# A gated attention and token mixer on one core: heads once a batch in 64x64 tiles, the last row group from transposed blocks, casting loads, and another end

## The chip, the core and the metric

The kernel runs on one core of a Trainium2 chip. TensorE (PE) multiplies matrices into PSUM; PEld is its loading of weights. VectorE (DVE), ScalarE (ACT) and GpSimd (POOL) work on elements, and SyncE (SP) issues most DMAs. The metric is the time of one execution on the device in microseconds, the median of several runs.

## The reference

Two stages for 8 batches of S = 3200 rows with D = 256; z has 64 columns and d_hyper is 64:

```python
scores = (1/S) * z @ z.T                    # per batch, 3200 x 3200, symmetric
x = u * (np.maximum(scores, 0.0) ** 2 @ v)  # 3200 x 256
wq, wk = x @ w_q, x @ w_k                   # 3200 x 64 each
W_tok = (1/8) * wq @ wk.T                   # 3200 x 3200
mixed = W_tok @ x
out = np.maximum(mixed, 0.0) @ w_out        # 3200 x 256
```

The second stage has no nonlinearity between `wq`, `wk` and `x`, so `mixed` is computed as `wq @ (wk.T @ x)`. The 64x256 matrix `wk.T @ x` of a batch is called its heads.

## The kernel before

**Tiling.** A batch has 25 row tiles of 128 rows, in seven row groups: six of four tiles (512 rows, groups 0 to 5) and a last one of a single tile (group 6, `LASTG`). The attention block of row group gi against row tile ti is computed transposed: `scores` multiplies z by z (64 rows of contraction, so two blocks run on the two row halves of TensorE at once) into the PSUM tile `sc`; `first_stage` takes the positive part into `g` on DVE or ACT; `second_stage` squares it into the fp16 tile `at` on POOL or ACT. Eleven `at` tiles go round. `second_product` multiplies `at` by `v` and adds up in `acc` (two banks), and `gate` multiplies by `u` into `x_sb`.

**Symmetric blocks.** The scores are symmetric, so some blocks are not computed but turned: `is_turned(gi, gj)` names pairs of groups of which the block of gi is transposed by a DMA on SP's queue (`second_stage`, the tile `tt`) and used for gj. Before, these are the next two groups, and group 4 for group 0; the last group has none and computes all its 25 blocks, four of 128x128 to a PSUM bank.

**Steps.** A main loop runs in steps (`k`). A step makes the scores of up to three pairs of blocks, runs the element stages of the pairs of the step before, and adds 4 to 25 row tiles into `acc`. Into this stream other work is woven: a call for keys (`keys_and_heads`), a mix (`mix`, TensorE tile `mx`), or an output projection (`project`, tile `fo`). The order is written by the program: `key_due`, `mix_due` and `shares` decide what goes into which step, and `at_phase` holds the loads that are due at a step. Most matmuls are cut into two of 64 rows of contraction, one for each row half (lane), in two passes so that each lane uses one PSUM bank at a time (`first_pass`, `second_pass`). Where there are no new scores left, near the end, matmuls are whole.

**Second stage.** `turn_x` transposes `x` by DMA. `keys_and_heads` makes queries and keys of a group (512 columns into one bank), `turn_keys` transposes the keys by DMA into `kx`, whose other 64 columns are zero. In a later key call `heads` multiplies the keys of a group that is done by its x, in the other bank, and `heads_out` adds the part to `ha` on DVE. After the last group of a batch the heads are copied to both halves (`spread_heads`), and six mixes and the projections of the batch are put into the steps of the next batches. The last group's mix and projection ride in key calls (`side_mix`, `side_proj`).

**Loads.** `load_piece` loads a piece of `v` or `z` in fp32 on SP's queue into `piece` and, some steps later, POOL and ACT in turn cast it to fp16 (`asides`). Only the first batch's `v` is loaded by casting DMAs of POOL's queue. `u` is loaded and the output stored on SP's queue.

**End.** The order after the last step is a list of words (`ENDING`). The last two groups' heads don't wait for turned keys: the Gram product of x (`last_gram`, tile `xtx`) is copied to fp32 and multiplied by w_k (`last_heads`).

Of the kernel before, what the change touches and what calls it, by code (L numbers as in the profile page):

```python
# [16 lines left out]
def kernel(  # L17
# [24 lines left out]
    LAG = 2  # L42
    FAR = 2
# [30 lines left out]
    def acc_tile(half, name, dtype=FP32):  # L74
# [9 lines left out]
        f00s H G g0A g1D f01 L F004AS f10s f11 F104AS h f20a q0s m01 m00 r00A F202DS r01D f21  # L84
        m10 q1a r10A m11 p00s F222DS p01 P002DS r11A p10a p11 P102DS P122DS P022AS m20 r20A
        p20s p21 m21 P204DS r21A p30s p31 P304DS s0a p40s p41 P422DS P402AS p60s P601AS p50a
        p51 P502AA P522DS
# [52 lines left out]
    def load_piece(k, b, src, dst, n0, nn, later):  # L140
        d = src.shape[2]
        piece = pst.tile([P, nn, d], FP32, tag="piece", name="piece")
        nc.sync.dma_start(out=piece[:], in_=rows(src, b)[:, n0 : n0 + nn, :])

        def cast():
            copy = nc.gpsimd.tensor_copy if now[0] % 2 == 0 else nc.scalar.copy
            copy(out=dst()[:, n0 : n0 + nn, :], in_=piece[:])

        due(k + later, lambda: asides.append(cast))
# [6 lines left out]
    def load_z(k, b, n0, nn):  # L156
        load_piece(k, b, z, lambda: zr, n0, nn, 4)

# [39 lines left out]
    wk2 = consts.tile([P, ND, 2, dh], FP32, tag="wk2", name="wk2")  # L198
    wo = consts.tile([P, ND, D], FP16, tag="wo", name="wo")
    zeros = consts.tile([P, P], FP16, tag="zeros", name="zeros")  # L200
    kxs = [pk.tile([P, 4, 2, dh], FP16, tag=f"kx{i}", name=f"kx{i}") for i in range(4)]
# [31 lines left out]
    def is_turned(gi, gj):  # L233
        return gi < gj < LASTG and (gj <= gi + FAR or (gi, gj) == (0, 4))

# [10 lines left out]
    for b in range(B):  # L246
        for gi in range(NG):
            near = [t for t in range(NT) if is_turned(gi, group_of(t))]
# [55 lines left out]
    def second_stage(p0, g, on_act):  # L304
# [15 lines left out]
        for b, gi, gj, n0, nn, c0, c1 in blocks:  # L320
            if (b, gi, gj) not in turned:
                bufs = {1: 3, 2: 4, 4: 1}[gj - gi]
                turned[b, gi, gj] = ptt.tile(
                    [P, 4, 4, P], FP16, tag=f"tt{gj - gi}", name=f"tt{gj - gi}", bufs=bufs
                )
# [140 lines left out]
    def gate(b, gi):  # L466
# [14 lines left out]
        else:  # L481
            if nn > 2:
# [3 lines left out]
            if nn > 2:  # L486
                nc.gpsimd.tensor_mul(out=x[:, n : 2 * n], in0=upper[:], in1=ug[:, n : 2 * n])  # L487
        to_turn.append((b, gi))
# [13 lines left out]
    def projections(b, gi, w, out, start=True):  # L502

        gw = widths[gi]
        return [
            Item(
                out=out,
                lhsT=lambda r, ac=ac: w[r, ac, :, :].rearrange("p t h -> p (t h)"),
                rhs=lambda r, ac=ac: xTs[b, gi][r, 0 : gw // P, ac, :],
# [3 lines left out]
            for ac in range(ND)  # L513
        ]

    def projections_out(b, gi, out):
# [5 lines left out]
        nc.scalar.copy(out=qks[b, gi][:, 0:gw], in_=out)  # L522
# [14 lines left out]
    def heads(b, gis, ps, stop=True):  # L537

        parts = [(gi, n) for gi in gis for n in range(widths[gi] // P)]
        return [  # L540
            Item(
                out=ps[:, 1, 0:D],
                lhsT=lambda r, gi=gi, n=n: ks[b, gi][r, n, :, :].rearrange("p a h -> p (a h)"),
                rhs=lambda r, gi=gi, n=n: xs[b, gi][r, n, :],
                start=((gi, n) == parts[0]),
                stop=(stop and (gi, n) == parts[-1]),
            )
            for gi, n in parts
        ]

    def heads_out(b, gis, ps):
        if gis[0] == 0:
            hacc[b] = psml.tile([P, D], FP32, tag="ha", name="ha")
            nc.vector.tensor_copy(out=hacc[b][0:dh, :], in_=ps[0:dh, 1, 0:D])
        elif gis[-1] < LASTG:
            nc.vector.tensor_add(
                out=hacc[b][0:dh, :], in0=hacc[b][0:dh, :], in1=ps[0:dh, 1, 0:D]
            )
        else:
            heads_done(b, ps[:, 1, 0:D], spread=False)  # L560
            to_spread.append(b)

    def spread_heads(b):
        nc.scalar.copy(out=hss[b][dh:P, :], in_=hss[b][0:dh, :])
        nc.scalar.copy(out=hz[b % 2][dh:P, :], in_=hss[b][0:dh, :])

    def heads_done(b, part, spread=True):
        hss[b] = psml.tile([P, D], FP16, tag="hs", name="hs")
        nc.vector.tensor_add(out=hss[b][0:dh, :], in0=hacc.pop(b)[0:dh, :], in1=part[0:dh, :])
        if spread:  # L570
            nc.vector.tensor_copy(out=hss[b][dh:P, :], in_=hss[b][0:dh, :])

# [370 lines left out]
    while groups:  # L943
# [34 lines left out]
        if mixing:  # L978
            mix_out(*mixing)
# [281 lines left out]
```

## Time and profile before

| | us |
|---|---|
| median of 3 runs | 780.81 |
| lowest and highest | 778.7, 783.08 |
| profiled execution, from first to last instruction | 776.9 |
| mean granted TensorE clock in it | 0.998 |

For the profiled execution the page gives the span; its own time, with what lies around the span, isn't listed apart from the runs, which are 1.8 to 6.2 us above that span.

How to read the lines of a profile: `L347 PE MATMUL acc<-v_sb,at 64*128 64x256 f16 x7334 | 472.5, 269 | 1.9 <-...` is a group of instructions: line of the kernel, engine, operation, output and inputs by the program's names, the weights' and the moving operand's form, the count; then busy microseconds and the mean nanoseconds of one; then the idle time of the engine just before them and what ended it. Matmuls are pipelined, so the length of one is longer than the distance to the next. A line of a timeline is start, length, and the instructions merged in it. `PEclk` is the granted share of the TensorE clock. The share of DMA is packet time over that of 16 engines and can go over 1. Line numbers are those of the kernel whose profile it is.

### The profile page before, as it was taken

The numbers are of one execution on the slowest core, as the hardware profiler recorded it, in microseconds if no ns is written. First come the engines' busy times: TensorE is split into PE (matmuls) and PEld (weight loads), VectorE is DVE, ScalarE is ACT, GpSimd is POOL, SyncE is SP. The second block draws the span as 40 slices with busy tenths as digits, with TensorE's granted clock in tenths as the row PEclk, the third lists the DMA queues.
The fourth block names the chain that finished last, engine by engine and source line by source line (L and its number), as shares of the span: only waits on it lengthen the run. The fifth ranks groups of instructions, "written<-read, shape, count | busy, mean of one in ns | idle before, by whom it ended". The sixth has DMA issues, their size and how long they took to land.

```text
span 776.9 us, 28324 instructions
## 1 busy us (share of the span) xinstructions
PE 765.0 (98%) x12542; PEld 629.3 (81%) x12542; DVE 474.0 (61%) x459; ACT 558.4 (72%) x657; POOL 554.1 (71%) x361
## 2 busy tenths in 40 slices
PE   9999999999999999999999999999999999999996
PEld 6777877888788988888888887888888888988884
DVE  7654676546765577555766457655585646665444
ACT  8666787777778787685867667758687878685465
POOL 7897797768766678766879668886777546875450
PEclk9999999999999999999999999999999999999999
DMA  8899799987999679994999949999489995987726
GB/s 186 176 202 227 141 212 173 191 181 125 213 220 216 133 188 204 234 229 134 189 224 231 220 131 203 226 202 242 115 210 187 217 236 112 206 190 160 161 65 259
DMA packets 276554, 147.03 MB, mean 189 GB/s; under 512 B 252112, under 2 KB 255696, under 8 KB 276432
## 3 DMA queue, kind: packets, MB, share of 16 engines
q1 hardware_dynamic: 275712, 143.33, 87.8%
q0 software_dynamic: 576, 1.64, 1.1%
q8 instruction: 98, 1.61, 0.9%
q14 instruction: 24, 0.20, 0.1%
q10 hardware_dynamic: 144, 0.26, 0.1%
HBM read 59.38 MB, written 26.21 MB: 110 GB/s over the span
## 4 chain that ended last, share of the span: by engine, by line
PE 92%; DVE 2%; ACT 2%; POOL 1%; DMA 1%; issue 1%; ACTq 0%; DVEq 0%; POOLq 0%
PE acc L347 67%; PE sc L285 12%; PE qk L347 6%; PE fo L347 5%; PE mx L600 1%; POOL at L310 1%; DMA tt<-at 1%; DVE g L299 1%; DVE x_sb L485 1%; ACT at L308 1%; DVE fo L1219 0%; ACT g L297 0%; DMA z<-in_z_dram 0%; ACT gt L484 0%; DVE zT L136 0%
## 5 line engine op out<-in xcount | busy, mean ns | idle before, releaser
L299 DVE TENSOR_SCALAR g<-sc 128x1024 f32<-128x1024 f32 x337 | 410.1, 1223 | 242.1 <-PE sc L285 220.8
L310 POOL TENSOR_TENSOR at<-g 128x1024 f16<-128x1024 f32 x238 | 448.1, 1893 | 122.2 <-DVE g L299 93.6
L347 PE MATMUL acc<-v_sb,at 64*128 64x256 f16 (+1 forms) x7387 | 479.5, 269 | 2.0 <-DVE x_sb L485 0.7
L347 PEld LDWEIGHTS <-at 64*128 64x128 f16 (+1 forms) x7387 | 370.2, 94 | 84.3 <-PE acc L347 24.5
L308 ACT ACTIVATE at<-g 128x1024 f16<-128x1024 f32 x230 | 239.3, 1055 | 27.2 <-DVE g L299 16.0
L347 PE MATMUL acc<-v_sb,tt 64*128 64x256 f16 (+1 forms) x2540 | 179.2, 269 | 0.0
L285 PE MATMUL sc<-zT 64*128 64x512 f16 (+1 forms) x1104 | 170.3, 345 | 0.9 <-DVE g L299 0.5
L297 ACT ACTIVATE g<-sc 128x1024 f32<-128x1024 f32 x131 | 134.1, 1023 | 41.6 <-PE sc L285 39.5
L347 PEld LDWEIGHTS <-tt 64*128 64x128 f16 (+1 forms) x2540 | 129.5, 94 | 15.2
L487 POOL TENSOR_TENSOR x_sb<-gt,u_sb 128x512 f16<-128x512 f32 x48 | 61.2, 1275 | 71.5 <-ACT gt L484 56.6
L621 ACT ACTIVATE rt<-mx 128x1024 f16<-128x1024 f32 x47 | 47.9, 1024 | 30.8 <-PE mx L600 30.5
L285 PEld LDWEIGHTS <-zT 64*128 64x128 f16 x1104 | 57.3, 94 | 10.9 <-issue 3.2
L484 ACT COPY gt<-acc 128x512 f32<-128x512 f32 x48 | 28.1, 586 | 48.4 <-PE acc L347 48.2
L347 PE MATMUL fo<-wo,rt 64*128 64x256 f16 (+1 forms) x688 | 58.6, 270 | 0.0
L347 PE MATMUL qk<-x_sb,kx 64*128 64x256 f16 x368 | 55.7, 269 | 0.6 <-DVE g L299 0.6
L522 ACT CAST qk<-qk 128x512 f16<-128x512 f32 x47 | 27.5, 585 | 35.9 <-PE qk L347 35.8
L485 DVE TENSOR_TENSOR x_sb<-acc,u_sb 128x512 f16<-128x512 f32 x48 | 33.1, 690 | 26.1 <-PE acc L347 24.7
L347 PEld LDWEIGHTS <-rt 64*128 64x128 f16 (+1 forms) x688 | 36.6, 94 | 14.3 <-PE fo L347 5.2
L682 ACT ACTIVATE fo<-fo 128x1024 f32<-128x1024 f32 x39 | 39.9, 1023 | 4.3 <-PE fo L347 4.3
L347 PEld LDWEIGHTS <-kx 64*128 64x128 f16 (+1 forms) x386 | 35.7, 94 | 5.1 <-PE qk L347 0.2
L347 PE MATMUL qk<-xT_sb,wqk 64*128 64x512 f16 (+1 forms) x94 | 27.9, 377 | 0.0
L347 PE MATMUL qk<-xT_sb,wkq 64*128 64x512 f16 (+1 forms) x90 | 26.7, 376 | 0.4 <-ACT g L297 0.4
(79 smaller groups left out, 243.3 us busy)
## 6 DMA issues: line engine op xcount, KB each, us to landing
u_sb<-in_u_dram SPq DMA_DIRECT2D x48, 512.0 KB, 5.1
out_dram<-fo SPq DMA_DIRECT2D x43, 512.0 KB, 3.5
piece<-in_v_dram SPq DMA_DIRECT2D x42, 512.0 KB, 4.6
piece<-in_z_dram SPq DMA_DIRECT2D x7, 512.0 KB, 5.3
tt<-at SPq DMA_TRANSPOSE x162, 4.8
out_dram<-fo SPq DMA_DIRECT2D x9, 256.0 KB, 3.1
piece<-in_z_dram SPq DMA_DIRECT2D x7, 288.0 KB, 6.1
u_sb<-in_u_dram SPq DMA_DIRECT2D x8, 128.0 KB, 3.1
```

The costliest lines, as they stand in the source:

```text
L285: nc.tensor.matmul(out=sc[:, h, at : at + w], lhsT=zT[b][half : half + dqk, ds(z_at(b, h) + ti * P, P)], rhs=zT[b][half : half + dqk, ds(z ...
L297: nc.scalar.activation(out=g[:], in_=sc[:], func=RELU, scale=GSCALE)
L299: nc.vector.tensor_scalar(out=g[:], in0=sc[:], scalar1=0.0, scalar2=GSCALE, op0=AOP.max, op1=AOP.mult)
L308: nc.scalar.square(out=out, in_=g[:])
L310: nc.gpsimd.tensor_mul(out=out, in0=g[:], in1=g[:])
L347: return nc.tensor.matmul(out=self.out, lhsT=self.lhsT(rows), rhs=self.rhs(rows), start=start, stop=stop)
L484: nc.scalar.copy(out=upper[:], in_=accs[1][:])
L485: nc.vector.tensor_mul(out=x[:, 0:n], in0=accs[0][:, 0:n], in1=ug[:, 0:n])
L487: nc.gpsimd.tensor_mul(out=x[:, n : 2 * n], in0=upper[:], in1=ug[:, n : 2 * n])
L522: nc.scalar.copy(out=qks[b, gi][:, 0:gw], in_=out)
L621: nc.scalar.activation(out=out, in_=ps[:], func=RELU)
L682: nc.scalar.mul(out=flat_out[:, sl], in_=part, mul=FINAL_SCALE)
```

## The change

- The scores of the last row group: all six of its blocks against the other groups are now turned by DMA (new tiles `ttl`, seven of them), and group 5's against group 2 is turned in place of group 4's against group 0. The last group computes only its own corner.
- Heads: all keys of a batch stand in one tile (`keys`, two of them), and the heads of the batch are one block of 50 matmuls, three steps after its last key call, each on a quarter (64x64) of TensorE. The even row tiles add up in one half of the partitions and the odd ones in the other; `heads_out` and `join_heads` add the four parts. `x_sb` has nine buffers for that, not seven, and `g` six, not seven.
- Keys: groups 0 and 1, 2 and 3, and 5 and 6 share a call; each lane has half of the columns.
- Loads: `v` and `z` of the later batches are casting DMAs on POOL's queue, straight into the fp16 tiles. `piece`, the casts and their list are gone.
- End: heads of groups 0 to 4 of the last batch go ahead of its last group; the other two groups' keys are multiplied from the transposed x (the last group's is transposed on TensorE), copied, and multiplied by x. The order of `ENDING` and the way a mix's output is split are new.

The diff, cut to its core:

```diff
+    SMALL = 6
+    MORE = {(2,5)}
+    HEADS_AFTER = 3
...
-    px = ctx.enter_context(tc.tile_pool(name="px", bufs=7))
+    px = ctx.enter_context(tc.tile_pool(name="px", bufs=9))
-    pst = ctx.enter_context(tc.tile_pool(name="pst", bufs=3))
-    pg = ctx.enter_context(tc.tile_pool(name="pg", bufs=7))
+    pg = ctx.enter_context(tc.tile_pool(name="pg", bufs=6))
...
-    def load_v(k, b, n0, nn):
+    def load_v(b, n0, nn):
         if n0 == 0:
             vs[b] = pv.tile([P, NT, D], FP16, tag="v_sb", name="v_sb")
-        load_piece(k, b, v, lambda: vs[b], n0, nn, 4 if b == 1 else 5)
+        nc.gpsimd.dma_start(out=vs[b][:, n0 : n0 + nn, :], in_=rows(v, b)[:, n0 : n0 + nn, :])
+    def load_z(b, n0, nn):
+        nc.gpsimd.dma_start(out=zr[:, n0 : n0 + nn, :], in_=rows(z, b)[:, n0 : n0 + nn, :])
...
     def is_turned(gi, gj):
-        return gi < gj < LASTG and (gj <= gi + FAR or (gi, gj) == (0, 4))
+        if gj == LASTG:
+            return gi < SMALL
+        return gi < gj < LASTG and (gj <= gi + FAR or (gi, gj) in MORE)
...
     def turn_keys(b, gi):
         gw = widths[gi]
         mine = slice(0, dh) if swapped(gi) else slice(dh, P)
-        kxs.append(kxs.pop(0))
-        ks[b, gi] = kxs[-1]
         nc.sync.dma_start_transpose(
-            out=ks[b, gi][:, 0 : gw // P, 0, :],
-            in_=qks[b, gi][mine, 0:gw],
+            out=keys[b % 2][:, ds(starts[gi] // P, gw // P), :], in_=qks[b, gi][mine, 0:gw]
         )
...
-    def heads(b, gis, ps, stop=True):
+    def heads(b, upto):
+        ps = ps_tile("hd")
+        for n0 in range(0, upto, 2):
+            for lane, rows_ in enumerate((LOW, HIGH)):
+                for n in range(n0, min(n0 + 2, upto)):
+                    gi = group_of(n)
+                    nc.tensor.matmul(
+                        out=ps[(LOW, HIGH)[n % 2], lane, 0:D],
+                        lhsT=keys[b % 2][rows_, n, :],
+                        rhs=xs[b, gi][rows_, n - starts[gi] // P, :],
+                        start=(n < 2),
+                        stop=(n >= upto - 2),
+                    )
+        return ps
+
+    def heads_out(b, ps):
+        part = psml.tile([P, D], FP32, tag="hb", name="hb", bufs=2)
+        nc.scalar.copy(out=part[:], in_=ps[:, 1, 0:D])
+        hacc[b] = psml.tile([P, D], FP32, tag="ha", name="ha", bufs=1)
+        nc.vector.tensor_add(out=hacc[b][:], in0=part[:], in1=ps[:, 0, 0:D])
+        after_step.append(lambda: join_heads(b))
...
     def group_done(k, b, gi):
-        if gi < LASTG - 1:
-            between(k + (5 if b + 1 < B else 3), lambda: keys_and_heads(b, [gi]))
+        if b + 1 < B and gi in (1, 3):
+            between(k + 5, lambda: make_keys(b, [gi - 1, gi]))
...
+        if not mixing and heads_at and min(heads_at.values()) <= k:
+            hb = min(heads_at)
+            del heads_at[hb]
+            n = min(n, 4)
+            pairs = pairs[: n // 2]
+            mixed_at[0] = k
+            hps = heads(hb, NT)
...
-                psg = [acc_tile(1, "xtx")[:, 0:D], ps_tile("xtx")[:, 0, 0:D]]
-                extra = [], lambda: last_gram(last, LASTG - 1, psg)
+                hps = heads(last, starts[LASTG - 1] // P)
+                heads_out(last, hps)
```

More of the change, by code (lines that the diff above doesn't have):

```diff
@@ L247 @@
         for gi in range(NG):
-            near = [t for t in range(NT) if is_turned(gi, group_of(t))]
+            near = [t for t in range(starts[LASTG] // P) if is_turned(gi, group_of(t))]
             own = [
@@ L607, in mix, with mix_out @@
         return ps
[L609 to L610 removed]
+    def mix_out(b, pair, db, ps, on_dve=False, which=ALL):
+        if (b, pair, "both") not in rts:
             both = prt.tile([P, 2, ND, W], FP16, tag="rt", name="rt")
@@ L1151 @@
         turn_x(*to_turn.pop(0))
-    assert len(fillers) == 3 and all(kb == last for kb, _ in keyed)
-    ps_, out_, g32 = {}, {}, {}
+    assert len(fillers) <= 3, len(fillers)
+    ps_, out_ = {}, {}
     def home(name, where):
@@ L1166, in ending @@
             what, n, more = word[0], int(word[1:2] or 0), word[2:]
-            if what == "H":
-                ps_["hd"] = ps_tile("hd")
-                heads_ = heads(last, sum((kgis for _, kgis in keyed), []), ps_["hd"], stop=False)
-                for fn in whole([heads_]):
-                    fn()
-            elif what == "G":
-                last_gram(last, LASTG, psg)
-            elif what == "g":
-                g32[n] = pg.tile([P, D], FP32, tag="g", name=f"G{n}")
-                (nc.scalar.copy if more == "A" else nc.vector.tensor_copy)(out=g32[n][:], in_=psg[n])
-            elif what == "L":
-                last_heads(last, g32, ps_["hd"])
+            if what in "fF" and n >= len(fillers):
+                continue
```

324 lines of the change are left out of this document (170 added, 154 removed).

## The prediction

> **What bounds the kernel now.** I read the page first: the span, the engines' busy time, the chain that ended last.
>
> ```profile
> span 776.9 us, 28324 instructions
> ...
> PE 765.0 (98%) x12542; PEld 629.3 (81%) x12542; DVE 474.0 (61%) x459; ACT 558.4 (72%) x657; POOL 554.1 (71%) x361
> ...
> PE 92%; DVE 2%; ACT 2%; POOL 1%; DMA 1%; issue 1%; ACTq 0%; DVEq 0%; POOLq 0%
> ```
>
> TensorE is busy 98% of the span and carries 92% of the chain. A busy TensorE need not be a full one, so I looked next at stretches by window (length, then busy us with counts of PE, weight loads, DVE, ACT, POOL; granted clock, DMA share, GB/s), and at its timeline near the end of the last batch.
>
> ```profile
> 200.00:240.00 40.00, 40.00 (x670) 33.21 (x668) 24.95 (x24) 30.09 (x35) 26.03 (x17) 1.00 1.15 215
> 360.00:380.00 20.00, 19.84 (x339) 16.73 (x335) 13.03 (x13) 16.12 (x19) 13.78 (x11) 1.00 0.46 90
> ```
>
> ```profile
> 745.23 0.61 PE L285 MATMUL sc<-zT 64*128 64x128 f16 x16
> 745.68 0.82 PE L347 MATMUL acc<-v_sb,at 64*128 64x256 f16 x12
> ...
> 747.86 1.47 PE L347 MATMUL acc<-v_sb,at 64*128 64x256 f16 x24
> 749.17 0.59 PE L600 MATMUL mx<-qk,hs 64*128 64x512 f16 x4
> 749.70 0.39 PE L347 MATMUL acc<-v_sb,at 128*128 128x256 f16 x2
> ...
> 750.80 1.04 PE L347 MATMUL fo<-wo,rt 128*128 128x256 f16 x8
> 751.67 0.38 PE L347 MATMUL acc<-v_sb,tt 128*128 128x256 f16 x2
> ```
>
> The start of each row against the next gives the pace. 24 half-height matmuls (64 rows, 256 columns) take 749.17 - 747.86 = 1.31 us, 54.6 ns each; eight full-height ones take 0.87 us, 109 ns each. Two halves run beside each other on the two row halves ("lanes") in the time of one whole. In mid-batch TensorE is busy 40.00 of 40.00 us, while VectorE (24.95), ScalarE (30.09) and GpSimd (26.03) all have room. So the bound is the number of columns that TensorE must stream; work taken off the other engines buys nothing by itself. DMA is the one resource that is also near full in part of a batch (share 1.15), and slack in another (0.46).
>
> **The change part by part.** The order of the instructions of both kernels gives the counts.
>
> *Last row group turned.* Per batch the 128-wide group is now read from six transposed 128x512 blocks, and only its corner is computed: 224 score matmuls of 128 columns become 32. From the rows above, 16 take 745.68 - 745.23 = 0.45 us, 28 ns each. 192 x 28 ns = **-5.4 us**, all on the bound engine. The products with v stay the same in number of columns; 152 half matmuls become 76 whole ones, 2 x 54.6 ns against 109 ns, nothing.
>
> *Heads in 64x64 tiles.*
>
> ```profile
> L347 PEld LDWEIGHTS <-kx 64*128 64x128 f16 x382 | 35.3, 94 | 5.1 <-PE qk L347 0.2
> ```
>
> Before, 382 half matmuls (as many as the loads of `kx`), half of their 128 weight columns zero, woven into the key calls: 382 x 54.6 ns = 20.9 us. After, 390 matmuls on a 64x64 quarter each (50 in each of seven batches, 40 in the last), written so that each four in a row hit the four quarters. No row shows a quarter. The bounds: four at a time, 390 / 4 x 109 ns = 10.6 us (-10.3); one after another, 390 x 109 ns = 42.5 us (+21.6). Below 10.6 it can't go, as each quarter still streams 256 columns. The nearest row is the halves: splitting the array in two gave two streams at full pace, so I take four, **-10.3 us**.
>
> The trace shows a weight load of 94 ns in the row above beside a matmul every 54.6 ns, so loads overlap matmuls on lanes. The Trainium skill (TensorEngine Tiling, "Restrictions and Gotchas") speaks against this part: column tiling can't be combined with Fast Weight Load; and TensorE: Matmul & The Clock Gate, "LDWEIGHTS (loading the stationary operand)", prices a load at its columns over 1.2 GHz, an estimate of 53 ns for 64 columns. Were the four loads of a quartet to run one after another, that would give 390 x 53 ns = 20.7 us, no gain; no run here shows it yet.
>
> Each of the eight blocks enters and leaves the new tile form. The nearest row: four `mx` of 512 columns from 749.17 should end their turn after 4 x 109 ns at 749.61, and the first full-height matmul starts at 749.70, so a change of form costs 0.09 us. 16 x 0.09 = **+1.5 us** (0 to three times that). Scores of one pair fewer stand in such a step and are made up later: nothing. The sum of the two halves leaves through one ScalarE copy and one VectorE add on engines with room.
>
> *Keys of two groups per call.* The same columns, now 256 wide on both lanes. The small group's key matmuls double from 28 to 56 and don't get cheaper than the 28 ns above: **+0.8 us**. Fewer calls mean fewer bank changes; I count nothing for it.
>
> *Casting loads.*
>
> ```profile
> L310 POOL TENSOR_TENSOR at<-g 128x1024 f16<-128x1024 f32 x238 | 448.1, 1893 | 122.2 <-DVE g L299 93.6 <-issue 8.8 <-DMA tt<-at 8.1
> ...
> L112 POOL DMA_DIRECT2D v_sb<-in_v_dram x4 | 2.3, 579 | 0.1
> ```
>
> 63 loads of v and z leave SP's queue and go out on GpSimd's as 64 issues x 0.58 us = 37 us; 21 fewer `at` products take 21 x 1.893 = 39.8 us off GpSimd, and the casts go too, from GpSimd and ScalarE, which I don't count. What stands behind a load on its queue is the next `at` product, 0.58 us later, covered by the 122.2 us of idle in its row. Worth on the path: 0. If that cover were gone, the 37 us would count against the 39.8 us removed, still no loss.
>
> *SP's queue.*
>
> ```profile
> L329 SPq DMA_TRANSPOSE tt<-at x162: 1194/1552/4160, 13.1 to 727.7; - x162
> ...
>   ACT at L308: 10.3, 7
>   POOL at L310: 9.8, 6
> ...
> DMA to landing us min/median/max: 2.5/4.8/8.5
> ...
> L143 SPq DMA_DIRECT2D piece<-in_v_dram x49: 332/570/1630, 41.4 to 636.3; - x49
> ...
> L143 SPq DMA_DIRECT2D piece<-in_z_dram x14: 423/436/822, 28.4 to 574.9; - x14
> ```
>
> 48 more transposes at 1.19 to 1.55 us are 57 to 74 us of issue time; 49 x 0.57 + 14 x 0.44 = 34 us go. Net +23 to +40 us on a queue that in mid-batch issues nearly back to back:
>
> ```profile
> 212.58 4.20 SPq L329 DMA_TRANSPOSE tt<-at x2
> 216.87 3.10 SPq L172 DMA_TRANSPOSE zT<-zr x2
> ```
>
> Behind a late transpose stand the reuse of the eleven `at` tiles (20.1 us of waits in all today) and, for the last group, its 24 turned blocks, the youngest of them made in the group just before. I count 0: the blocks land in 4.8 us, 8.5 at worst, and are read one to two steps of 776.9 / 169 = 4.6 us later (the kernel runs in 169 such steps); the shifted block (2,5) for (0,4) leaves the crowded start of a batch. The bound on it is the third rival.
>
> *End.*
>
> ```profile
> 756.26 0.71 PE L347 MATMUL acc<-v_sb,at 128*128 128x256 f16 x5
> 756.80 0.60 PE L347 MATMUL fo<-wo,rt 128*128 128x256 f16 x4
> ...
> 758.41 1.13 PE L587 MATMUL hd<-G,wk 128*128 128x256 f32 x4
> 759.38 1.47 PE L347 MATMUL fo<-wo,rt 128*128 128x256 f16 x12
> ...
> 761.21 0.70 PE L600 MATMUL mx<-qk,hs 64*128 64x512 f16 x4
> ```
>
> From the last accumulation (756.80) to the first mix (761.21) are 4.4 us. The fp32 product (759.38 - 758.41 = 0.97 us), ten Gram and four heads matmuls go; ten key matmuls of 128 columns, two transposes and five heads matmuls come, 1.2 us less on TensorE. The new chain (gate, transposes, copy, keys, copy, heads, add) has as many hops. One projection of 512 rows more is out before it, so its output is not in the tail. **-1 us**, between -3 and +3.
>
> Sum: -5.4 - 10.3 + 1.5 + 0.8 - 1.0 = **-14.4 us**. Span 776.9 - 14.4 = 762.5. The three runs (778.7 to 783.08) lie 1.8 to 6.2 us over the profiled span, their median 3.9; I add that: **766.4 us**.
>
> **The rivals.** (1) *Quarters run two at a time*, by a shared row stream or by their weight loads: 390 / 2 x 109 = 21.3 us, 10.7 us more than counted: 777.1 us, at the edge of no change. By the load price of the Trainium skill's page on TensorE, above, it would be 776.5. For it: no row shows a column split. Against: the halves scale fully. Chance 0.18.
>
> (2) *Quarters run one after another*: 31.9 us more, 798 us. A group of 50 heads would then stand about 5.5 us, as a block in which nothing else streams. Chance 0.08.
>
> (3) *SP becomes the bound; it ends on the other side.* The place is the first two thirds of a batch, where DMA is at 1.15. If half of the upper price, 20 us, reaches the path, as half of the time is slack: 766.4 + 20 = 786.4 us, slower. It decides from the point where waits of `at` on transposes outgrow GpSimd's idle there (40 - 26.0 = 14 us in 40); then the products are late, then scores. Against it: 20.1 us of such waits today, and TensorE at 40.00 of 40.00 all the same; all loads gone from that queue. Chance 0.18.
>
> **How the numbers follow.** Forecast 0.56. A measurement of this kernel tells about 0.5%, 3.9 us, from no change, so faster means under 776.9 and slower over 784.7. Faster: 0.55 of the forecast, half of (1) 0.09, light cases of (3) 0.03: 0.67. Same: 0.01 + 0.09 + 0.03 = 0.13. Slower: (2) 0.08 and the rest of (3) 0.12: 0.20. Range: down to 758 (no cost of changing form, the end at -3, and 5 of the 11.9 us in which TensorE isn't busy), up to 787, which holds (1) and the half price of (3); left out are (2) and the full price of (3). The forecast's own range is 758 to 773.
>
> **What would show it.** Right: the 128-column scores at 32, heads matmuls starting every 27 ns in blocks of 1.4 us, TensorE still busy 97% and more, waits of `at` on transposes near 20 us. Wrong: heads starts 55 or 109 ns apart; gaps before `acc` matmuls released by a `ttl` or `tt` landing; SP's transposes with a median well over 1.55 us.

## The result, and the profile after

The changed kernel takes 782.08 us (median of 20 runs, 779.14 to 786.51) against 778.74 us before (20 runs on the same chip): a ratio of 1.0041, 95% interval 1.0027 to 1.0056. I had forecast 766.4 us with a range of 758 to 787. The time is inside the range, whose upper end stood for the first rival and half of the third, but no gain came: the change costs 3 us, less than the 0.5% that I had called measurable. The profiled execution took 782.09 us, 1.8 us more than its span. In the experiments, runs more than 1.5% above the fastest of their kernel are left out of medians and ratios (with them the kernel that turns the last group in no batch has 781.38 us, not 779.9).

The page of the kernel after, in the rows that answer to those of before (each digit is a slice of 19.5 us; a queue's columns are packets, MB and share of 16 engines):

```profile
span 780.3 us, 28288 instructions
...
PE 755.8 (97%) x12541; PEld 609.0 (78%) x12541; DVE 444.0 (57%) x411; ACT 529.8 (68%) x637; POOL 519.4 (67%) x366
...
PEclk9998999899999999999999999999999999999999
...
q1 hardware_dynamic: 292464, 121.15, 83.0%
q0 software_dynamic: 9648, 15.98, 14.8%
...
PE 92%; DMA 3%; ACT 2%; DVE 1%; POOL 1%; issue 1%; SPq 0%; ACTq 0%; DVEq 0%
```

TensorE is busy 9.2 us less than before (755.8 against 765.0), yet the span is 3.4 us longer. DMA has 3% of the chain, where it had 1%. The clock row has an 8 in two slices, both in the first fifth; before it stood at 0.998 over the whole span, now at 0.989.

The groups of instructions that the change is about, by shape (busy us, mean ns of one, idle of the engine before them):

```profile
L551 PE MATMUL hd<-x_sb,keys 64*64 64x256 f16 x376 | 12.2, 274 | 5.8 <-DMA keys<-qk 5.8
L551 PEld LDWEIGHTS <-keys 64*64 64x64 f16 x390 | 10.4, 107 | 7.8 <-DMA keys<-qk 6.1 <-issue 1.7
L274 PE MATMUL sc<-zT 64*128 64x128 f16 x32 | 3.1, 216 | 0.0
```

The work is as forecast: 376 heads matmuls (14 more are the last group's) in 12.2 us of busy time, the 128-column scores down to 32. The idle time before the heads, 5.8 us, is one wait.

Stretches by window (length; busy us and counts of PE, PEld, DVE, ACT, POOL; clock, DMA share, GB/s): the two slices with the low clock, one in mid-kernel beside them, and then a close look at 5 us right after the second stall and 5 us later.

```profile
60.00:80.00 20.00, 14.70 (x216) 11.47 (x212) 6.95 (x7) 12.05 (x15) 12.81 (x10) 0.83 1.15 193
140.00:160.00 20.00, 14.12 (x219) 10.15 (x216) 6.02 (x7) 7.92 (x10) 7.72 (x6) 0.83 1.02 171
400.00:420.00 20.00, 20.00 (x356) 16.30 (x354) 11.59 (x11) 13.92 (x18) 15.24 (x12) 1.00 1.04 179
```

```profile
151.00:156.00 5.00, 4.80 (x44) 2.96 (x46) 1.65 (x2) 3.66 (x5) 2.20 (x2) 0.50 0.86 155
157.00:162.00 5.00, 5.00 (x90) 4.07 (x88) 1.94 (x2) 2.67 (x5) 1.50 (x1) 1.00 1.37 177
```

TensorE stands still for 5 to 6 us in each of the first two windows, and afterwards runs at a granted clock of 0.50, 44 matmuls in 5 us where it then does 90. So a stall costs more than its length.

**The first stall**, in the timeline (start, length, instructions; in brackets the idle time before and what ended it):

```profile
63.19 1.06 ACT L297 ACTIVATE at<-g 128x1024 f16<-128x1024 f32 x1 [3.62 <-DMA tt<-at]
...
65.49 3.75 POOL L299 TENSOR_TENSOR at<-g 128x1024 f16<-128x1024 f32 x2 [3.00 <-DMA ttl<-at]
65.86 0.83 ACT L167 COPY zT<-zT 64x768 f16<-64x768 f16 x1 [1.62 <-DMA zT<-zr]
...
68.22 1.06 ACT L297 ACTIVATE at<-g 128x1024 f16<-128x1024 f32 x1 [1.53 <-DMA tt<-at]
69.18 1.01 ACT L286 ACTIVATE g<-sc 128x1024 f32<-128x1024 f32 x1
...
70.24 0.61 PE L337 MATMUL qk<-xT_sb,wqk 64*128 64x256 f16 x4 [5.30 <-ACT g L286]
```

Read it from the bottom. The first key call has no PSUM tile, because the copy of `sc` into `g` (L286) is late. That copy stands in ScalarE's order behind `at` (L297) and the copy of `zT`. `at` waits for a free tile, which it is when a transpose of the old one has landed; three transposes in a row were late. TensorE pays 5.30 us.

**The second stall**, the heads of batch 0:

```profile
133.13 0.59 ACT L532 CAST qk<-qk 128x512 f16<-128x512 f32 x1
...
144.09 1.29 PE L551 MATMUL hd<-x_sb,keys 64*64 64x256 f16 x40
144.68 1.98 SPq L319 DMA_TRANSPOSE ttl<-at  x1
...
146.75 1.20 SPq L537 DMA_TRANSPOSE keys<-qk  x1
148.05 1.18 SPq L537 DMA_TRANSPOSE keys<-ql  x1
...
151.20 0.64 PE L551 MATMUL hd<-x_sb,keys 64*64 64x256 f16 x8 [5.82 <-DMA keys<-qk]
```

The 40 matmuls whose keys are there run 26 ns apart ((1.29 - 0.27) / 39). The other ten need the keys of groups 5 and 6. ScalarE had copied those of group 5 by 133.72, but SP issued their transpose only at 146.75, 13.0 us later, behind the transposes ahead of it. TensorE reached the heads at 144.09, found no keys, and waited 5.82 us.

The sum closes. The two stalls are 5.3 + 5.8 us. At half clock after them stand 4.1 us (70.24 to about 74.4) and 5.1 us (151.20 to about 156.3), of which half is lost, 4.6 us. 780.3 - 15.7 = 764.6 us, against the forecast span of 762.5.

### The profile page after: what moved, and what is told of

Same layout as the page of the kernel before. It is cut to its first block, busy times and chain, and to the rows that moved or that the text cites. A ratio compares the mean times of both kernels' runs of the same rounds, so it can differ in the third digit from the quotient of the medians.

```text
span 780.3 us, 28288 instructions
## 1 busy us (share of the span) xinstructions
PE 755.8 (97%) x12541; PEld 609.0 (78%) x12541; DVE 444.0 (57%) x411; ACT 529.8 (68%) x637; POOL 519.4 (67%) x366
## 4 chain that ended last, share of the span: by engine, by line
PE 92%; DMA 3%; ACT 2%; DVE 1%; POOL 1%; issue 1%; SPq 0%; ACTq 0%; DVEq 0%
PE acc L337 69%; PE sc L274 11%; PE fo L337 5%; PE qk L337 3%; DMA tt<-at 1%; PE hd L551 1%; DVE x_sb L476 1%; PE mx L608 1%; DMA keys<-qk 1%; DMA zT<-zr 1%; ACT g L286 1%; POOL at L299 0%; ACT gt L475 0%; PE sc L902 0%; ACT fo L1255 0%
## 5 line engine op out<-in xcount | busy, mean ns | idle before, releaser
L288 DVE TENSOR_SCALAR g<-sc 128x1024 f32<-128x1024 f32 x319 | 387.9, 1223 | 257.8 <-PE sc L274 231.8
L299 POOL TENSOR_TENSOR at<-g 128x1024 f16<-128x1024 f32 x217 | 409.5, 1895 | 162.3 <-DVE g L288 113.3
L337 PE MATMUL acc<-v_sb,at 64*128 64x256 f16 (+1 forms) x6979 | 452.6, 271 | 3.8 <-DVE x_sb L476 0.9
L337 PEld LDWEIGHTS <-at 64*128 64x128 f16 (+1 forms) x6979 | 338.8, 94 | 98.7 <-PE acc L337 29.8
L297 ACT ACTIVATE at<-g 128x1024 f16<-128x1024 f32 x227 | 235.9, 1056 | 39.3 <-DMA tt<-at 23.1
L286 ACT ACTIVATE g<-sc 128x1024 f32<-128x1024 f32 x125 | 127.8, 1022 | 56.9 <-PE sc L274 55.0
L274 PE MATMUL sc<-zT 64*128 64x512 f16 (+1 forms) x912 | 159.8, 373 | 1.1 <-ACT g L286 0.9
L628 ACT ACTIVATE rt<-mx 128x1024 f16<-128x1024 f32 (+1 forms) x46 | 45.0, 987 | 28.6 <-PE mx L608 28.3
L274 PEld LDWEIGHTS <-zT 64*128 64x128 f16 x912 | 47.3, 94 | 10.4 <-issue 3.0
L145 POOL DMA_DIRECT2D v_sb<-in_v_dram x49 | 28.9, 591 | 0.0
L337 PE MATMUL qk<-xT_sb,wqk 64*128 64x256 f16 (+1 forms) x188 | 19.0, 275 | 5.3 <-ACT g L286 5.3
L337 PE MATMUL acc<-v_sb,ttl 64*128 64x256 f16 (+1 forms) x360 | 23.6, 269 | 0.0
L337 PEld LDWEIGHTS <-ttl 64*128 64x128 f16 (+1 forms) x360 | 21.2, 94 | 0.5
```

Of the source, the lines that this page charges most:

```text
L145: nc.gpsimd.dma_start(out=vs[b][:, n0 : n0 + nn, :], in_=rows(v, b)[:, n0 : n0 + nn, :])
L274: nc.tensor.matmul(out=sc[:, h, at : at + w], lhsT=zT[b][half : half + dqk, ds(z_at(b, h) + ti * P, P)], rhs=zT[b][half : half + dqk, ds(z ...
L286: nc.scalar.activation(out=g[:], in_=sc[:], func=RELU, scale=GSCALE)
L288: nc.vector.tensor_scalar(out=g[:], in0=sc[:], scalar1=0.0, scalar2=GSCALE, op0=AOP.max, op1=AOP.mult)
L297: nc.scalar.square(out=out, in_=g[:])
L299: nc.gpsimd.tensor_mul(out=out, in0=g[:], in1=g[:])
```

## The experiments

All times are medians of interleaved runs beside the kernel before, which had 778.25 to 778.74 us there. A trace is that of one execution, the first of its kernel, and can lie some us from the median (785.34 against 781.06 us with batch 0's keys one group per call), so the length of a stall in it is not a mean.

| kernel | us | ratio to before, 95% |
|---|---|---|
| changed kernel | 782.08 | 1.0027 to 1.0056 |
| batch 0's heads two steps later | 780.23 | 0.9993 to 1.0031 |
| seven casting loads left out | 776.74 | 0.9962 to 0.9996 |
| batch 0 doesn't turn the last group | 779.83 | 0.9990 to 1.0045 |
| seven loads later in batch 0 | 777.85 | 0.9978 to 1.0009 |
| batch 0 doesn't turn block 2,5 | 774.20 | 0.9877 to 0.9944 |
| block 0,4 in place of 2,5 | 779.6 | 0.9984 to 1.0046 |
| batch 0's keys one group per call | 781.06 | 1.0003 to 1.0043 |
| no last group turned in batch 0, later heads | 775.56 | 0.9918 to 0.9964 |
| the same, and seven loads left out | 767.73 | 0.9812 to 0.9887 |
| no last group or block 2,5 in batch 0 | 776.9 | 0.9951 to 0.9997 |
| **the same, and later heads** | **768.44** | **0.9818 to 0.9873** |
| no block 2,5 in batch 0, later heads | 770.95 | 0.9844 to 0.9905 |
| the same, and loads later | 769.33 | 0.9841 to 0.9910 |
| last group turned in no batch, rest as in bold | 779.9 | 0.9991 to 1.0040 |
| the same with seven `g` buffers | 779.93 | 0.9981 to 1.0036 |
| three blocks of the last group | 783.8 | 1.0014 to 1.0080 |
| the same with seven `g` buffers | 780.6 | 1.0001 to 1.0065 |
| before, with casting loads alone | 780.55 | 1.0001 to 1.0057 |

**One relief at a time.** My theory was that the SP queue's transposes are late; its rival, that the casting loads are dear in themselves.

Heads of batch 0 two steps later:

```diff
-                heads_at[b] = now[0] + HEADS_AFTER
+                heads_at[b] = now[0] + HEADS_AFTER + 2 * (b == 0)
```

> Edit: the heads of batch 0 are made two steps later (five steps after its last key call, not three). Theory: the saving on TensorE is there as forecast, and two stalls in the first two batches, each with a stretch of half clock behind it, take it back; the second (5.8 us before the heads of batch 0 at 151 us, with some 3.4 us of lost clock) is a wait for the transposed keys. Two steps more cover it: about 9 us less, 773 us. Rival, the block in 64x64 tiles itself costs what is missing: 782 us, no change. Rival, the stall only moves to the next late transpose: 780 to 783 us.

Measured 780.23 us, not 773. Its timeline says why:

```profile
153.70 1.50 PE L551 MATMUL hd<-x_sb,keys 64*64 64x256 f16 x48
...
158.86 1.06 ACT L297 ACTIVATE at<-g 128x1024 f16<-128x1024 f32 x1 [10.89 <-DMA tt<-at]
159.82 1.01 ACT L286 ACTIVATE g<-sc 128x1024 f32<-128x1024 f32 x1
...
160.88 0.61 PE L274 MATMUL sc<-zT 64*128 64x512 f16 x2 [5.57 <-ACT g L286]
```

The heads no longer wait. But the queue is as late as before, and now ScalarE waits 10.89 us for an `at` tile and TensorE 5.57 us for ScalarE. The stall was moved, not removed: the keys were only the first to need what the queue owed.

Seven casting loads left out: batch 1 reads batch 0's `v`.

```diff
+        if b == 1:
+            vs[b] = vs[0]
+            return
```

> Edit: the casting loads of v for batch 1 are left out, batch 1 reads batch 0's v (so its output is another one); seven of 64 loads less, all in the stretch of the first stall. Theory that the casting loads crowd out the transposes in batch 0: the first stall (5.3 us at 65 to 70 us, and its lost clock) goes, about 773 us. Theory that the added transposes of the last row group do it: 781 to 782 us, no change.

Measured 776.74 us. The stall at 70 us shrank from 5.3 to 2.4 us, the one at the heads stayed at 5.7. Both theories were half right.

The kernel before with nothing but the casting loads (the two `load_piece` calls in `load_v` and `load_z` replaced by `nc.gpsimd.dma_start`):

> Edit: the kernel before with the casting loads alone. If the casting loads crowd out the transposes, a stall shows in batch 0 here too: 784 to 788 us against 778.7. If it is the added transposes: 778.7 us within 1.5 us, as the engines that get rid of casts are not the bound.

Measured 780.55 us, 2.0 us slower than before (interval 1.0001 to 1.0057, so only just told from no change), with its clock at 0.999 and no stall over 1 us. The loads may have a small price of their own, which I had at 0, but alone they don't make the stalls.

Batch 0 turns nothing of the last group (`is_turned` is handed the batch):

```diff
-            return gi < SMALL
+            return gi < SMALL and b > 0
```

> Edit: the changed kernel, but batch 0 computes the last row group's blocks itself, as before; six of 48 added transposes go, and 24 score matmuls of 128 columns come back (0.7 us). Theory that the added transposes make the at tiles late in batch 0: the first stall goes, about 774 us. Theory that the casting loads do it: 782 to 783 us.

Measured 779.83 us: both stalls were smaller (4.0 and 2.9 us), and neither was gone.

**Where the place of the work is not the cause.** From here on the expectations weigh two theories. Theory Q: SP's in-order queue of transposes is over its capacity from 40 to 160 us, and whatever waits for its end stalls TensorE. Theory K: the queue has room, and keys and heads stand in the wrong places. The first batch's keys one group per call, as before:

```diff
+        if b == 0 and gi < 4:
+            between(k + 5, lambda: make_keys(b, [gi]))
-        if b + 1 < B and gi in (1, 3):
+        elif b + 1 < B and gi in (1, 3):
```

> The changed kernel, but the first batch's groups 0 to 3 have a key call each as in the kernel before, so TensorE has key work from some 50 us on. Theory Q: the transposes are the same, so the stall at 70 us moves or stays, 5 us in sum, and the one at 146 us stays: 780 to 783. Theory K: with the keys spread as before the stall at 70 us goes with its half clock (5.3 and 3.4 us), the one at 146 us stays: 772 to 774.

Measured 781.06 us, with stalls of 6.2 and 7.3 us in the trace. That refutes the theory that the pairing of the keys is to blame for the first stall. The other shift, the block that is turned:

```diff
-    MORE = {(2,5)}
+    MORE = {(0, 4)}
```

> The changed kernel, but the block of groups 0 and 4 is turned as in the kernel before, not that of groups 2 and 5, in all batches. If the move of that block is what overfills 40 to 70 us: as without it in batch 0 (774.2) or better, 770 to 775. If the stretch from 20 to 40 us is as full (SP 0.97 there), the queue starts later work late all the same, and the time stays at 779 to 783.

Measured 779.6 us, with the interval of its ratio overlapping that of the changed kernel: the move of the block is worth 2 or 3 us at most, and is not the cause either.

**Reliefs together.** No last group turned in batch 0, and its heads later:

> The changed kernel with two reliefs at once: batch 0 doesn't turn the last row group's blocks, and its heads come two steps later. Theory Q (SP's in-order queue of transposes is over its capacity from 40 to 160 us, and whatever waits for its end stalls TensorE; a stall is moved unless transposes are taken out): alone they gave 779.8 and 780.2; the heads no longer wait (2.9 us and its 0.8), the stall at 70 us stays (4.0), part of the heads' stall comes back at the `at` tiles: 774 to 777. Theory K (keys and heads in wrong places, the queue has room): the heads' stall goes without a successor and only the one at 70 us stays: 770 to 773.

Measured 775.56 us, as the queue theory had it: a stall of 3.9 us at 70 and one of 2.1 us at 159. To this, the seven loads left out:

> Three reliefs at once: batch 0 doesn't turn the last group's blocks, its heads come two steps later, and batch 1 reads batch 0's v, so seven casting loads are left out (its output differs). Theory Q: fewest bytes in the critical stretch; stalls 1 to 3 us in all, the time 768 to 772, at best the forecast's 766. Theory K: as with the first two alone, 770 to 773. If the stalls go and the time still stays above 776, the forecast's TensorE terms were wrong too.

Measured 767.73 us, 7.8 us less, with SP's list of DMAs unchanged. The two traces show how loads of GpSimd's queue reach a queue of SP, in the DMA view from 40 to 70 us (share of 16 engines; for the issues the count and the median us to landing). First with the loads, then without:

```profile
q1 hardware_dynamic: 12475, 4.08, 88.9%
q0 software_dynamic: 576, 1.05, 22.0%
...
tt<-at SPq DMA_TRANSPOSE x10, 5.5
```

```profile
q1 hardware_dynamic: 16194, 5.47, 108.6%
...
tt<-at SPq DMA_TRANSPOSE x11, 4.4
```

Without the loads the hardware queue moves 16194 packets in place of 12475, and a transpose lands in 4.4 in place of 5.5 us. So loads on GpSimd's queue slow the transposes of SP's; that the place where they meet is the 16 DMA engines is the likely reading, though GpSimd's own time for issuing the loads (0.59 us each) was not separated from it. The sums are close, 110.9% and 108.6%, but 110% isn't a ceiling. The best kernel below, in the same 30 us:

```profile
q1 hardware_dynamic: 13015, 4.41, 89.1%
q0 software_dynamic: 641, 1.18, 32.7%
...
tt<-at SPq DMA_TRANSPOSE x8, 6.8
```

Its sum is 121.8%, its transposes land later, and it doesn't stall there. It has fewer of them, 8 against 10, but the kernel without the loads has 11 and doesn't stall there either. So neither the share, nor the time to land, nor the number of transposes tells by itself whether TensorE stalls.

The same without leaving anything out, the loads of `v` in steps 15 to 21:

```diff
-                at = k + (9 + 5 * i // 3 if b == 0 else 4 + 2 * i)
+                at = k + (14 + i if b == 0 else 4 + 2 * i)
```

> The changed kernel, but the seven casting loads of the next batch's v in batch 0 are issued in steps 15 to 21 in place of 10 to 20 (some 60 to 95 us in place of 40 to 90), nothing left out. If the limit at 70 us is the DMA engines that loads and transposes share: the stall there falls from 5.3 us to about 2.4 as with the loads left out, with less half clock, the one at 146 us stays: 776 to 779. If only SP's own issuing counts, GpSimd's loads don't matter: 781 to 783. A new stall before batch 1's first products (near 100 us), where these loads are read, would show up as more.

Measured 777.85 us, and the DMA view of 40 to 70 us:

```profile
q1 hardware_dynamic: 15823, 4.94, 93.2%
q0 software_dynamic: 144, 0.26, 7.7%
...
tt<-at SPq DMA_TRANSPOSE x9, 4.1
```

4.2 us are back for moving seven loads by up to 20 us. If SP's own issuing were all that counts, the loads would not have mattered. The stall at 70 fell to 3.8 us, less than expected; the one at the heads stayed (5.5 us).

Fewer transposes in batch 0, all loads kept:

```diff
-        return gi < gj < LASTG and (gj <= gi + FAR or (gi, gj) in MORE)
+        return gi < gj < LASTG and (gj <= gi + FAR or ((gi, gj) in MORE and b > 0))
```

> Batch 0 turns neither the last group's blocks nor the block of groups 2 and 5, and its heads come two steps later; all casting loads stay. Against the kernel with the first two alone SP has some two to four transposes of 512x512 fewer between 40 and 100 us, 2 us each. Theory Q: the stall at 70 us shrinks by 2 us or more and the successor at 150 us too: 768 to 773, 3 us or more below the kernel with the first two alone. Theory K: that block costs TensorE 4 score matmuls of 512 columns more, 0.4 us, and gives nothing: the same time as that kernel.

Measured **768.44 us** (last group and block 2,5 not turned in batch 0, heads later), a ratio to the kernel before of 0.9845, interval 0.9818 to 0.9873. It beats both kernels. Its page and the two windows:

```profile
span 765.0 us, 28355 instructions
...
PE 752.4 (98%) x12569; PEld 608.1 (79%) x12569; DVE 447.7 (59%) x414; ACT 532.1 (70%) x640; POOL 526.5 (69%) x370
...
PEclk9999999999999999999999999999999999999999
```

```profile
60.00:80.00 20.00, 19.88 (x346) 16.06 (x342) 12.43 (x12) 15.89 (x20) 15.89 (x12) 1.00 1.21 189
140.00:160.00 20.00, 19.13 (x340) 15.32 (x340) 8.79 (x9) 11.99 (x15) 13.74 (x10) 1.00 1.05 175
```

No stall over 0.7 us, no slice under full clock, and a span 2.5 us from the forecast's. The parts of it one by one: block 2,5 alone,

> The changed kernel, but batch 0 doesn't turn the block of groups 2 and 5; all else stays (last group turned, heads three steps after the keys, casting loads). Theory Q: what is too much is the transposes between 40 and 70 us, and a few fewer of 2 us each before 70 us free the `at` tiles in time: the stall there (5.3 us) goes with its half clock (some 2 us); the one at 146 us stays or shrinks by the 2 to 3 us that the queue is earlier: 771 to 775. If it takes all three reliefs together (rival T, a plain sum of transposes over the whole stretch, with no place of its own), 779 to 781, as each relief alone gave.

774.20 us, inside what theory Q gave, but not in its way: in the trace the stall at 70 us, which was to go, is still 3.5 us long, and the one at the heads, which was to stay, is gone. Block 2,5 and later heads,

> As the kernel without that block in batch 0, and batch 0's heads two steps later; the last group is turned in batch 0 too. Theory Q: the stall at 70 us gone, and the one at 146 us either gone or back at the `at` tiles near 155 us with up to 3 us: 767 to 772. Rival T: 776 to 778.

770.95 us, with a stall of 2.8 us left at 66 and no half clock after it. Last group and block 2,5, but the heads at their old place,

> As the kernel at 768.4 us, but batch 0's heads stay three steps after the keys. Theory Q: the stall at 70 us is gone, the keys' turn is issued a few us earlier than in the changed kernel, so TensorE waits 0 to 3 us for it at 146 us: 768 to 771. If the two steps are what matters there (theory K): 774, the 5.8 us and the half clock back.

776.9 us, a miss of 6 us to the theory of the queue: here TensorE waits as long as in the changed kernel, although batch 0 has eight transposes fewer.

```profile
146.27 2.06 SPq L537 DMA_TRANSPOSE keys<-qk  x1
148.42 1.18 SPq L537 DMA_TRANSPOSE keys<-ql  x1
...
151.16 0.64 PE L551 MATMUL hd<-x_sb,keys 64*64 64x256 f16 x8 [5.71 <-DMA keys<-qk]
```

The copy of these keys ends 4.4 us earlier than in the changed kernel (129.33 against 133.72), but their transpose is issued hardly earlier (146.27 against 146.75): it stands 16.9 us behind the copy. With block 2,5 alone left out it was issued 11.3 us behind (143.38 against 132.08), and the heads, also at their old place, did not wait. So fewer transposes removed the wait at the heads in one kernel and not in the other. That batch 1's transposes stand in the queue by then may be the reason; it was not tested. With two steps more distance the heads waited in no kernel that was run. The two steps, which alone moved the stall elsewhere, are worth some 8 us here.

All three shifts with the last group turned in every batch and nothing left out (block 2,5 out of batch 0, later heads, later loads):

> Three shifts in batch 0 and nothing left out: the block of groups 2 and 5 not turned there, heads two steps later, the loads of v later; the last group is turned in every batch. Without the shift of the loads it gave 771.0 with 2.8 us of stall near 69 us left. If DMA sharing is that rest: 766 to 768.5, the forecast's 766.4 with the 1 us that the block and small gaps cost. If SP's issuing alone: 771.

Measured 769.33 us, the runs between 765.55 and 772.02, so it can't be told from the best kernel, nor from the 770.95 without the shift of the loads; its profiled execution has no stall over 0.6 us and a span of 763.8 us.

**What turning the last group is worth.** The best kernel, but with the last group turned in no batch:

> As the kernel at 768.4 us (neither the last group's blocks nor block 2,5 turned in batch 0, heads later there), but no batch turns the last group's blocks, so each computes its 128-wide score products itself. My forecast's term: 6.4 us for turning them in all five batches, of which four are left in that kernel: 4.3 us by sc128 alone, so 772 to 773. If TensorE gains nothing from it in mid-batch because something else is the limit there, 768; if the transposes cost more than they save in batches 1 to 4, 765 to 767.

Measured 779.9 us, 11 us more by the medians and 13 by the ratios to the kernel before; I had expected 4.3. (That text counts five batches; there are eight, and 168 of the 128-column scores come back in seven of them.) And with seven `g` buffers, as the kernel before had, in place of six:

> As the kernel that turns none of the last group (781.4), with seven g buffers. If g buffers are the room: the small stalls in mid-batch and the one at 70 us go: 771 to 774, the 768.4 of the kernel with the turns in seven batches and 4.9 us of scores. If not: 780 to 782.

Measured 779.93 us, so the buffers are not the reason. The page of this last kernel:

```profile
span 776.1 us, 28713 instructions
...
PE 758.1 (98%) x12789; PEld 612.5 (79%) x12789; DVE 463.6 (60%) x428; ACT 541.0 (70%) x649; POOL 562.3 (72%) x389
```

Of the 11.1 us of span between it and the best kernel, TensorE's work is 758.1 - 752.4 = 5.7 us, near the 168 x 28 ns = 4.7 of the scores. The other 5.4 us are time in which TensorE isn't busy (18.0 against 12.6). The turned blocks also take 36 us of `at` products and the like off GpSimd (562.3 against 526.5). That those short gaps come from GpSimd was not tested, so more than half of what turning the last group is worth has no shown cause.

The last pair asks whether the `g` buffers were the room that the change took away. The base, three blocks of the last group in place of six (`SMALL = 3`):

> The changed kernel with the last group turned against groups 0 to 2 only, three blocks per batch in place of six. By the forecast's prices 84 score matmuls of 128 columns come back in seven batches, 2.4 us; some three transposes of 1.3 us less per batch. If these blocks are what overfills the queue: 778 to 780, as with batch 0's six left out (779.8) and 2 us of TensorE; if not: 783 to 785. It is the base for the next kernel.

Measured 783.8 us; and with `pg` at seven buffers:

> As the kernel with three blocks, but with seven g buffers in place of six, as in the kernel before. If the seventh buffer is the room that was lost: ScalarE and VectorE empty PSUM ahead of a late `at` tile, the stall at 70 us shrinks from 5 us to 2 or less and its half clock goes, the one at 146 us stays or shrinks: 4 to 8 us below the kernel with three blocks. If the queue of transposes is all that counts, the same time within 2 us.

Measured 780.6 us, in the trace with 4.6 us of stall left at 70 and none over 1.3 us at the heads. The intervals overlap (1.0014 to 1.0080 and 1.0001 to 1.0065): the seventh buffer may be worth some us, and it doesn't remove the stall at 70.

## Why the prediction was wrong

**The step that failed is SP's queue, "I count 0": the runs show 15.7 us.** I took the time of a block from issue to landing, 4.8 us, and set it against one to two steps. What counted was the time from the data being ready to the issue, and the trace of before had it (timeline of before):

```profile
53.25 0.59 ACT L522 CAST qk<-qk 128x512 f16<-128x512 f32 x1
...
66.76 1.20 SPq L529 DMA_TRANSPOSE kx<-qk  x1
...
143.07 0.58 ACT L522 CAST qk<-qk 128x512 f16<-128x512 f32 x1
...
151.13 1.21 SPq L529 DMA_TRANSPOSE kx<-qk  x1
...
178.62 0.38 PE L347 MATMUL qk<-x_sb,kx 64*128 64x256 f16 x2
```

Keys copied at 53.84 are issued at 66.76: 12.9 us behind. Those of batch 0's last groups are 7.5 us behind (143.65 to 151.13), but their heads came only at 178.62, 35 us after the copy. The change put the heads 10.4 us after it (133.72 to 144.09). The queue became later by some 5 us, and the deadline came 25 us nearer; the second is what I left out when I costed "heads once a batch" by its matmuls alone.

**Rival 3 had the mechanism, not the place or the price.** I put the late `at` tiles into two thirds of every batch and 20 us on the path. The runs show two places, in batch 0 and the first steps of batch 1 (the second at the keys, which that rival doesn't name), and nothing of it in mid-kernel, where the window at 400 us is full. There the price is 15.7 us, of which 4.6 is the half clock, which was in none of my cases.

After the stalls of 5.3 and 5.8 us the granted clock was 0.50 from 67.56 to 74.39 and from 149.48 to 156.31. By the Trainium skill (TensorE: Matmul & The Clock Gate, "Part 1: The HAM clock gate"), the clock halves after an idle window of about 3.4 us and comes back after a busy one, and these windows run freely, whatever the kernel does. The trace agrees: both stretches are 6.83 us, two windows of 3.41, and their starts are 81.92 us apart, 24 windows. In all twenty traces a half clock inside the kernel lasts 3.41, 6.83 or 10.24 us. The runs add that a window need not be idle throughout. Two stalls, cut at the edges of these windows (length, busy time of each engine, clock, DMA); first one of 2.4 us (seven loads left out), then one of 2.8 us (block 2,5 out, later heads):

```profile
63.28:66.69 3.41, 1.17 (x20) 0.79 (x17) 1.21 (x2) 1.86 (x2) 0.32 (x1) 1.00 0.86 168
66.69:70.11 3.42, 3.26 (x30) 2.37 (x31) 1.23 (x1) 3.37 (x6) 2.68 (x3) 0.50 0.83 162
```

```profile
63.51:66.93 3.42, 2.33 (x40) 1.67 (x35) 1.92 (x2) 0.33 (x1) 2.20 (x2) 1.00 1.20 157
66.93:70.34 3.41, 1.72 (x30) 1.38 (x31) 0.78 (x1) 3.36 (x5) 1.22 (x2) 1.00 0.99 207
```

The shorter stall lies in one window, which is idle for 2.2 us, and the next window has half the clock. The longer one is split by an edge into 1.1 and 1.7 us and costs no clock. Over all traces, each full-clock window with 2.06 us or more of idle TensorE was followed by half clock and none with 1.96 us or less was, but for one in the first 10 us of a run. So where a stall falls against the windows is luck.

**"Loads leave SP's queue: 0 on the path"** looked at the queues one by one and not at what they share. Moving the loads from one queue to another left them in the way of the transposes: perhaps 2.0 us in the kernel before, and 4.2 us back in the changed one when they come later. "The shifted block leaves the crowded start" mattered little and the wrong way: 779.6 us with it put back.

**TensorE's terms were right as work, but not term by term in the time.** Heads: forecast four at a time, 27 ns apart; the trace has 26, so rivals 1 and 2 are out, and with them the case in which loads at the price of the Trainium skill (TensorE: Matmul & The Clock Gate, "LDWEIGHTS (loading the stationary operand)") run one after another and the heads gain nothing: here loads of 107 ns lie beside matmuls 26 ns apart. The scores of 128 columns: 32, as counted; 168 of them cost 4.7 us by my price and TensorE's work differs by 5.7. The end: from the last `acc` matmul to the end of the span 19.9 us before and 19.3 after, forecast -1. The change of tile form: 24 half-height matmuls from 142.69 should end their turn at 144.00, and the heads start at 144.09, 0.09 us as forecast. The small group's keys (+0.8) were priced too high. Their matmuls have 64 columns now, and four start between 219.96 and 220.02, 15 ns each, so the 56 cost no more than I had priced for the 28 before.

Once the stalls are gone the sum stands: spans of 765.0 and 763.8 us against 762.5 forecast, times of 768.4 and 769.3 against 766.4. But that the sum comes out is in part luck. With the last group turned in no batch and seven `g` buffers (776.1 us of span) the other parts together give 0.8 us against the kernel before, where their terms are worth 9.0: TensorE's work falls by 6.9 us and its idle time grows from 11.9 to 18.0. Turning the last group then gives 11.1 us of span where its scores were priced at 4.7, and the half that isn't TensorE's work is idle time that I can't explain.

**The 3.9 us around the span** were too many: the profiled executions lie 1.8 us above theirs (782.09 and 780.3), and the median of 20 runs of the kernel before was 778.74, not 780.81.

**What stays open.** The kernel before, with the casting loads and nearly as many bytes (5.35 MB against 5.52 from 40 to 70 us), has no stall at 70 us. Which part of the change took away its room there isn't settled: keys in pairs, the block's move, the last group's turns in batch 0, the seven loads and (with three blocks of the last group) the seventh `g` buffer were each tried alone, and none does it alone. TensorE has less work in batch 0 after the change and so comes earlier to each wait; that would fit, and was not tested by itself. The stall at 70 also differs between kernels that are the same up to there: 2.2 us (heads at their old place) and none (the best kernel), so its size hangs on small shifts in the time.

## What to carry to other kernels

Before a consumer is moved ahead, measure the time from its data being ready to the DMA's issue, not only from issue to landing; on an in-order queue that is close to full the first can be nearly three times the second (13.0 us for these keys, against a median of 4.8 us from issue to landing in the kernel before), and a distance that looked like waste is the cover for it. A transfer that changes its queue can still slow what stays on the old one (a transpose landed in 5.5 us with the loads and in 4.4 without): look at all queues in the stretch in question, not over the span, and don't take a share of some 110% for the ceiling. Where a gain on the bound engine doesn't show, look at the first batches apart from the rest, and price a stall with the slow clock after it; some transposes fewer and two steps more distance in one batch of eight gave back 13.6 us.

## What the runs showed of the hardware

- Four 64x64 quarters of TensorE, each with weights of its own for every matmul, ran at 26 to 27 ns per matmul of 256 columns, with weight loads of 107 ns beside them.
- The granted clock of TensorE changed only at the edges of windows of 3.41 us: stretches at 0.50 inside the kernel lasted 3.41, 6.83 or 10.24 us in twenty traces. A window with 2.06 us or more of idle TensorE was followed by half clock, one with 1.96 us or less wasn't (one exception, 1.6 us idle in the first 10 us of a run). So a stall of 2.4 us cost clock and one of 2.8 us, split by an edge, did not.
- Casting loads on GpSimd's queue slow transposes on SP's: in the same 30 us a transpose landed in 5.5 us with the loads (88.9 + 22.0% of the DMA engines' time) and in 4.4 without (108.6%). A share of 110% is not a limit: another kernel had 121.8% there and no stall.
